# Diagonal sums of the sixth chunk on GpSimd, state scaling and the sums' copy on ScalarE, and a new order for the first chunks and weight loads

## The chip, the cores and the metric

The kernel runs on one core of one Trainium2 chip. The metric is the device time of one execution in microseconds (us). The kernel before was timed three times: 413.6, 413.74 and 414.51 us, median 413.74 us. The execution that was profiled took 413.68 us; from its first to its last instruction (the span, on which all times below are counted) are 412.0 us.

The engines are TensorE (PE: matmuls; PEld: its weight loads), VectorE (DVE), ScalarE (ACT), GpSimd (POOL) and SyncE (SP, which here only issues DMAs). Each works through its own instructions strictly in order.

## The reference

Two parts are chained. A linear attention with decay, per batch (4), head (8) and step (768), heads of width 48:

```
state = zeros(B, H, 48, 48)
for t in range(768):
    y[:, :, t] = r_t . (state + (u * k_t) outer v_t)
    state = w_t[:, None] * state + k_t outer v_t
```

Then, with x the 3072 rows of y with the heads side by side (384 wide), a gated layer: `h = max(x @ w1, x @ w2, x @ w3)` (768 wide), `out = h @ w_out`. Everything is float32; the weights w1, w2, w3 and w_out arrive as float64 bits.

## The kernel before, in words

The attention is cut into 24 chunks k of 128 steps (six per batch). A chunk has steps with one-letter names, and the number behind a letter is the chunk: `n` loads its r, k, w (tile `tin`, three buffers); `b`, `s`, `f` are VectorE's backward scan (L360), two tiny operations (L368, L369) and its forward scan (L374) of the decays; `r` scales r and k by them (L385, L386); `X` is the scores on TensorE (`gram`, L449); `T` transposes k (`tu`, L469, copied to `kn` by ScalarE, L471); `R` adds what comes from the state (L482); `U` makes the new state (L492, and L496, which adds the old one); `S` scales it by the decay `dec` into `sstar` (L507); `M` puts the scores under a mask into `a` (L458); `V` and `Z` multiply by v (L527); `E` copies the chunk's y into x (ScalarE, L545) and, after the third and fourth chunk, shifts 16-row pieces of x with six DMAs, three from SyncE's queue and three from ScalarE's (L554); `c` is a check of the decays on ScalarE (L391).

The diagonal term needs, per step and head, the sum over the width of u r k. For the first chunks (k < CS, here 6) step `d` multiplies r and k on VectorE (L399), `D` sums with small matmuls on TensorE (L411), and `e` copies the eight sums to `cs` (L419). For later chunks `d` is two multiplications on GpSimd of r, k and u loaded in another layout (`kr`, L402 and L403; u is `u_bc`), and `e` is a reduction on VectorE (L421). Either way GpSimd then spreads the sums over the diagonal of `a` (L427). Step `e` of chunk k also issues the load of v for chunk k+1 (and of `kr`, if it takes the GpSimd way) on SyncE's queue.

The layer works on halves of 512 rows (six in all). Every weight i of 24 takes a DMA (`w` or `load_w`, L287), one ScalarE operation (L303, it waits for the DMA) and two VectorE operations (L312, L314). For the first half plain float32 matmuls are used: the first two groups in two parts (L147 on 384 columns, L155 on the other 128), the rest whole (L167, six records a group). A group's sums lie in one of three `psm` buffers in turn (the sums of `D` and the warmers' matmuls use the same three), and are taken up one group later: the first by a copy on ScalarE (L130), the others by a maximum on VectorE (L133).

Order around the change: the string FRONT lists the first four chunks' steps one by one. `W4` is four warming matmuls on TensorE (L573) whose result nobody reads; `i` begins a weight (L303), `c` without a number begins and finishes one, `p` and `m` are a part or a group of matmuls of the layer, `w` loads a weight, `a` a unit of a later chunk. Each engine gets its part of this list in this order. SyncE's queue too: a DMA that must wait (for a buffer to come free, for x to be written, for an earlier DMA on one of the eight semaphores) holds up all behind it.

Of the kernel before, what the change touches and what calls it, by code (L numbers as in the profile page):

```python
# [34 lines left out]
ALU = mybir.AluOpType  # L35
AF = mybir.ActivationFunctionType
# [4 lines left out]
B, H, S, D = 4, 8, 768, 48  # L41
DM, FF = 384, 768
NP = 4
# [10 lines left out]
CPH = HT // C  # L54
# [12 lines left out]

FRONT = ("b0 s0 f0 d0 W2 D0 W3 r0 X0 T0 W3 c0 e0 b1 s1 d1 D1 U0 f1 W4 R0 e1 M0 V0 Z0 E0 S0 n3 r1 "  # L70
# [3 lines left out]
TURN = "b1 d1 w | f1 w | D1 r1 c1 | e1 M0 w | "  # L74
ORD = "w R0 V0 U0 X1 Z0 E0 b2 d2 | f2 n3 w | D2 S0 r2 c2 | e2 M1 w | T1 w | |"


START = ("mcamcamcamcamcamcaamca"
         "mcmacamcacammacmcamacamcamcamcamcamcaafafafaxmafmmammaaf")
CS = 6  # L80
LINE = 128
PLAIN = 1
CHECK = 2
# [11 lines left out]
def kernel(ctx: ExitStack, tc, tin, nat, u_flat, u_pair, v_t, w_all, out, ytr):  # L95
    nc = tc.nc
# [99 lines left out]
    with ExitStack() as fast:  # L196
# [23 lines left out]
        def load_nat(k):  # L220
            b, c = divmod(k, NCH)
            if k in natt:
                return
            vt = v_p.tile([128, DM], F32, name="v")
            kr = None
            if k >= CS:
                kr = nat_p.tile([128, 2, DM], F32, name="kr")
                nc.sync.dma_start(out=kr[:, :, :], in_=nat[b, c, :, 1:3, :])
            nc.sync.dma_start(out=vt[:, :], in_=nat[b, c, :, 0, :])
            natt[k] = (vt, kr)  # L230
# [39 lines left out]
        sstar = [cst.tile([128, NP, 64], F32, name=f"sstar{i}") for i in range(2)]  # L270
        dec = [cst.tile([128, LINE], F32, name=f"dec{i}")[:, 0:NP] for i in range(2)]
# [83 lines left out]
        prep = {k: {} for k in range(NK)}  # L355
# [37 lines left out]
        def prep_diag1(k):  # L393
            if k < CS:
                t = tbuf[k % NB]
                prep[k]["kr"] = n = nat_p.tile([128, 2, DM], F32, name="kr")[:, :, :].rearrange("p a b -> p (a b)")[:, 0:NP * C]
                n, r, q = (z.rearrange("p (a b) -> p a b", a=NP) for z in (n, t[:, WC:WC + NP * C], t[:, WC + NP * C:TC_]))
                for j in range(2):
                    nc.vector.tensor_tensor(out=pairs(n, j), in0=placed(r, j), in1=pairs(q, j), op=ALU.mult)  # L399
                return  # L400
            n = natt[k][1]
            nc.gpsimd.tensor_tensor(out=n[:, 0, :], in0=n[:, 0, :], in1=n[:, 1, :], op=ALU.mult)  # L402
            nc.gpsimd.tensor_tensor(out=n[:, 0, :], in0=n[:, 0, :], in1=u_bc[:, :], op=ALU.mult)  # L403

        def prep_diag_sum(k):
            if k < CS:
                n, t = prep[k]["kr"], tbuf[k % NB]
                prep[k]["ps"] = ps = ps_m.tile([128, HT], F32, name="psm")
                for pr in range(NP):
                    for lo in (0, HC):  # L410
                        nc.tensor.matmul(ps[lo:lo + HC, pr:2 * NP:NP], lhsT=n[0:112, pr * C + lo:pr * C + lo + HC],  # L411
                                         rhs=t[0:112, TC_ + 2 * pr:TC_ + 2 * pr + 2], start=(pr == 0), stop=True,
                                         skip_group_check=True)

        def prep_diag2(k):
            ahead("D", k)
            cs = small.tile([128, LINE], F32, name="cs")[:, 0:H]
            if k < CS:
                nc.vector.tensor_copy(out=cs[:, :], in_=prep[k]["ps"][:, 0:H])  # L419
            else:  # L420
                nc.vector.tensor_reduce(out=cs[:, :].rearrange("p (a b) -> p b a", a=2),  # L421
                                        in_=natt[k][1][:, 0, :].rearrange("p (b a d) -> p b a d", a=2, d=D),
                                        axis=AX.X, op=ALU.add)
            a = a_p.tile([128, 4, 3, HC], F32, name="a")
            for lo in (0, HC):
                rows = slice(lo, lo + HC)
                nc.gpsimd.affine_select(out=a[rows, :, 0:2, :], pattern=[[0, 4], [0, 2], [1, HC]],  # L427
                                        in_=cs[rows, :].rearrange("p (a b) -> p a b", b=2).unsqueeze(3).broadcast_to([HC, 4, 2, HC]),
                                        compare_op=ALU.is_equal, fill=0.0, base=0, channel_multiplier=-1)
            prep[k]["a"] = a  # L430
            if k + 1 < NK:
                load_nat(k + 1)
# [28 lines left out]
        def goes_on(k):  # L461
            return k % NCH < NCH - 1
# [36 lines left out]
        def state(k):  # L499

            if goes_on(k):
                new = prep[k]["pu"][0:112, 0:NP * D].rearrange("p (a b) -> p a b", a=NP)
                if k % NCH > 0 and k >= CPH:
                    cur = scur[0:112, :].rearrange("p (a b) -> p a b", a=NP)
                    nc.vector.tensor_tensor(out=cur, in0=new, in1=sstar[k % 2][0:112, :, 0:D], op=ALU.add)
                    new = cur
                nc.vector.tensor_tensor(out=sstar[(k + 1) % 2][0:112, :, 0:D], in0=new,  # L507
                                        in1=dec[(k + 1) % 2][0:112, :].unsqueeze(2).broadcast_to([112, NP, D]), op=ALU.mult)

        def after(later, sooner):  # L510

# [27 lines left out]
        def result(k):  # L539
# [11 lines left out]
            for lo in (0, 64) if cols else ():  # L551
                for j in range(KT):
                    eng = nc.scalar if lo and half < PLAIN else nc.sync
                    eng.dma_start(out=x[lo + 48:lo + 64, j, cols], in_=x[lo + 16 * j:lo + 16 * j + 16, KT, cols])  # L554

        steps = dict(X=scores, M=take, T=transposes, R=from_state, U=to_state, S=state, V=values, Z=values2, E=result, n=load,
                     b=prep_scan_b, s=prep_start, f=prep_scan_f, r=prep_rk, c=prep_check, d=prep_diag1,
                     D=prep_diag_sum, e=prep_diag2)
        ready = {("n", k) for k in range(3)}

        def ahead(step, k):

            if k < NK and (step, k) not in ready:
                ready.add((step, k))
                steps[step](k)
# [107 lines left out]
        def take_x(early=False):  # L673
            h = len(xs)
            there = ("E", CPH * (h + 1) - 2) in ready if early else units >= min(UPH * (h + 1) + XD, UPC * NK)
            if h < NH and there and groups >= GPH * h - 2 * CPH:
                xs[h] = x_parts(h)
# [39 lines left out]
        simple = dict(p=part, a=unit, c=weights, i=begin, w=load_w, m=group, f=fix, x=lambda: take_x(True))  # L717
        for step in FRONT.split():
            if step in simple:
# [14 lines left out]
    with tc.If(verdict[0] != 0, label="general"), ExitStack() as slow:  # L734
        pool = lambda name, bufs, **kw: slow.enter_context(tc.tile_pool(name=name, bufs=bufs, **kw))
        c1 = pool("c1", 1)
# [7 lines left out]
        with tc.For_i(0, B) as b:  # L744
            for pr in range(NP):
# [8 lines left out]
                for hh in range(2):  # L754
                    rows = slice(64 * hh, 64 * hh + 48)
                    for t, o in ((wt, pr * WS + 1), (rt, WC + pr * C), (kt, WC + NP * C + pr * C)):
                        for c in range(NCH):
                            for lo in (0, HC):
                                at = o + (HC - lo if t is kt and pr % 2 == 0 else lo)
                                nc.sync.dma_start(out=t[rows, c * C + lo:c * C + lo + HC],  # L760
                                                  in_=tin[ds(b, 1), c, rows, at:at + HC].rearrange("a p n -> (a p) n"))
                    nc.sync.dma_start(out=uc[rows, :], in_=u_pair[pr, hh])
                nc.vector.tensor_scalar(out=uk[0:112, :], in0=kt[0:112, :], scalar1=uc[0:112, :], scalar2=None, op0=ALU.mult)
                for j in range(KT):
                    with tc.For_i(0, 16) as i:
# [5 lines left out]
                        for hh in range(2):  # L771
                            nc.sync.dma_start(
                                out=vb[64 * hh:64 * hh + 48, :],
                                in_=v_t[ds(b, 1), 2 * pr + hh, ds(i + 16 * j, 1), :].rearrange("a e t -> (a e) t").broadcast_to([48, S]))
# [22 lines left out]
        for i in range(NW if w_all.dtype != F32 else 0):  # L797
# [5 lines left out]
            low, scale = raw[:, 0:2 * PC:2], sc[:, :].bitcast(F32)  # L803
# [16 lines left out]
        with tc.For_i(0, NH) as half:  # L820
            x = xs_p.tile([128, KT, HT], F32, name="x")
# [73 lines left out]
```

## Time and profile before

| what | value |
|---|---|
| median of three runs | 413.74 us |
| the profiled execution | 413.68 us |
| its span | 412.0 us |
| TensorE busy (matmuls) | 400.9 us, 97% |
| VectorE busy | 279.4 us, 68% |
| ScalarE busy | 151.3 us, 37% |
| GpSimd busy | 80.6 us, 20% |
| granted TensorE clock | 1.000 |

A line of the timeline gives the start in us, the duration, the engine, the line of the program, the operation, what it writes and reads, the shape, how many were merged, and in square brackets how long the engine sat idle before it and what ended that wait. "issue" is a wait that no semaphore in the profile explains. A line with SPq or ACTq is a DMA being issued. Matmuls overlap, so that busy time on TensorE includes time in the pipeline; merged lines of small matmuls end some 0.1 to 0.2 us after the next line starts.

### The profile page before, as it was taken

To read this page: it belongs to the slowest core of one execution; us is meant where nothing else is said; L and a number is where in the kernel's file an instruction comes from. 1 tells how busy PE (TensorE), PEld (TensorE's weight loads), DVE (VectorE), ACT (ScalarE), POOL (GpSimd) and SP (SyncE) were. 2 spreads that over 40 slices of the span, in tenths; PEclk is the share of its full clock that TensorE was granted. 3 is DMA by queue.
4 is the path that set the end of the run, shared out by engine and by line. 5 is a ranking of instruction groups with operands and counts; after the bars stand their busy time and mean duration, and the time that the engine had idled before them with its cause. 6 is when DMAs were issued, how large, how long until landed. Compare 5 with 4: busy or idle time off the path is not lost.

```text
span 412.0 us, 9165 instructions
## 1 busy us (share of the span) xinstructions
PE 400.9 (97%) x3729; PEld 315.6 (77%) x3729; DVE 279.4 (68%) x511; ACT 151.3 (37%) x318; POOL 80.6 (20%) x96
## 2 busy tenths in 40 slices
PE   6989999999999999999999999999999999999994
PEld 2656454556688889988889988889988888988894
DVE  6989999989869969848777658678666622233320
ACT  1344434233535532525433644433622321311211
POOL 2410032233222211213122212223123200000000
PEclk9999999999999999999999999999999999999999
DMA  8594994641550330595563686751550000300001
GB/s 210 157 324 143 335 312 140 208 139 40 152 176 23 105 111 17 139 286 163 176 184 113 158 267 212 228 154 43 180 168 2 0 2 2 97 1 0 2 15 66
DMA packets 24126, 54.09 MB, mean 131 GB/s; under 512 B 3312, under 2 KB 9776, under 8 KB 24080
## 3 DMA queue, kind: packets, MB, share of 16 engines
q1 hardware_dynamic: 20160, 43.43, 34.2%
q10 hardware_dynamic: 3920, 10.03, 8.1%
q8 instruction: 30, 0.49, 0.5%
q14 instruction: 16, 0.13, 0.1%
HBM read 47.55 MB, written 4.72 MB: 127 GB/s over the span
## 4 chain that ended last, share of the span: by engine, by line
PE 94%; DMA 1%; ACT 1%; issue 1%; SPq 1%; POOL 0%; POOLq 0%; ACTq 0%
PE psm L167 56%; PE psm L187 16%; PE gram L449 5%; PE y L527 5%; PE tu L492 3%; PE y L482 3%; PE psm L573 2%; PE tu L469 2%; DMA out_dram<-m 1%; PE psm L411 1%; PE psm L147 1%; SPq L554 1%; DMA x<-x 0%; PE psm L155 0%; PE tu L496 0%
## 5 line engine op out<-in xcount | busy, mean ns | idle before, releaser
L167 PE MATMUL psm<-x_hi,w 128*128 128x512 f32 x540 | 172.8, 394 | 0.2 <-ACT m L191 0.2
L167 PEld LDWEIGHTS psm<-x_hi,w 128*128 128x128 f32 x540 | 101.4, 188 | 22.0 <-ACT m L191 0.8
L167 PE MATMUL psm<-x_lo,w 128*128 128x512 f32 x270 | 105.3, 390 | 0.0
L133 DVE TENSOR_TENSOR m<-psm,m 128x512 f32<-128x512 f32 x60 | 41.1, 685 | 58.9 <-PE psm L167 44.5
L187 PE MATMUL psm<-w,h_hi 128*128 128x384 f32 x288 | 78.2, 364 | 0.0
L427 POOL TENSOR_SCALAR_AFFINE_SELECT a<-cs 64x512 f32<-64x512 f32 x48 | 37.1, 774 | 143.4 <-DVE cs L421 92.6
L167 PEld LDWEIGHTS psm<-x_lo,w 128*128 128x128 f32 x270 | 50.8, 188 | 9.8
L187 PEld LDWEIGHTS psm<-w,h_hi 128*128 128x128 f32 x288 | 51.8, 188 | 6.5 <-DVE w L314 0.4
L167 PE MATMUL psm<-x,w 128*128 128x512 f32 x96 | 42.6, 597 | 0.0
L545 ACT COPY x<-y 112x512 f32<-112x512 f32 x24 | 14.1, 586 | 75.2 <-PE y L527 74.7
L402 POOL TENSOR_TENSOR kr<-kr 128x384 f32<-128x384 f32 x18 | 21.1, 1172 | 99.8 <-PE y L527 88.5
L187 PE MATMUL psm<-w,h_lo 128*128 128x384 f32 x120 | 40.3, 336 | 0.0
L391 ACT ACTIVATE gf<-gf 112x1034 f32<-112x1034 f32 x24 | 25.7, 1070 | 35.6 <-DVE tin L386 35.2
L110 ACT CAST h_hi<-m 128x512 fp32r<-128x512 f32 x30 | 18.7, 622 | 53.7 <-DVE m L133 53.7
L374 DVE TENSOR_TENSOR_SCAN gf<-tin,d_fwd 112x517 f32<-112x517 f32 x24 | 36.1, 1502 | 0.7
L167 PEld LDWEIGHTS psm<-x,w 128*128 128x128 f32 x96 | 17.8, 190 | 20.4 <-issue 19.1
L360 DVE TENSOR_TENSOR_SCAN gf<-tin,d_bwd 112x517 f32<-112x517 f32 x24 | 29.9, 1246 | 4.8 <-DMA tin<-in_tin_dram 4.7
L111 DVE TENSOR_TENSOR h_lo<-m,h_hi 128x512 fp32r<-128x512 f32 x30 | 20.6, 688 | 16.7 <-ACT h_hi L110 16.7
L527 PE MATMUL y<-a,v 64*48 64x64 f32 (+3 forms) x768 | 25.7, 246 | 0.6 <-POOLq L534 0.2
L458 DVE COPY_PREDICATED a<-mask,gram 128x384 f32<-128x384 int32 x48 | 25.3, 581 | 0.5 <-PE gram L449 0.5
L527 PEld LDWEIGHTS y<-a,v 64*64 64x64 f32 (+1 forms) x768 | 21.6, 126 | 4.7 <-issue 3.1
L130 ACT COPY m<-psm 128x512 f32<-128x512 f32 x30 | 17.5, 582 | 16.4 <-PE psm L167 9.8
(72 smaller groups left out, 424.9 us busy)
## 6 DMA issues: line engine op xcount, KB each, us to landing
tin<-in_tin_dram SPq DMA_DIRECT2D x23, 448.0 KB, 5.1
w<-in_w_all_dram SPq DMA_DIRECT2D x24, 384.0 KB, 7.2
cv<-in_w_all_dram ACTq DMA_DIRECT2D x24, 384.0 KB, 3.6
kr<-in_nat_dram SPq DMA_DIRECT2D x18, 384.0 KB, 5.8
tin<-in_tin_dram SPq DMA_DIRECT2D x23, 231.0 KB, 3.5
v<-in_nat_dram SPq DMA_DIRECT2D x24, 192.0 KB, 5.5
out_dram<-m SPq DMA_DIRECT2D x24, 192.0 KB, 2.6
x<-x SPq DMA_DIRECT2D x30, 32.0 KB, 2.0
```

What stands on the lines that cost most here:

```text
L111: rest = lambda: nc.vector.tensor_tensor(out=lo, in0=src, in1=hi.bitcast(F32), op=ALU.subtract)
L133: nc.vector.tensor_tensor(out=m[:, :], in0=ps[:, :], in1=m[:, :], op=ALU.max)
L167: nc.tensor.matmul(ps[:, :], lhsT=wt[f * 3 + wi][:, ct * 128:(ct + 1) * 128], rhs=xt[:, ct, :], start=(n == 0), stop=(n == KT * len(terms) ...
L187: nc.tensor.matmul(pss[tt][:, 0:DM], lhsT=ht[f][:, tok], rhs=wt[FT * 3 + f][:, :], start=(f == 0 and i == 0), stop=(f == FT - 1 and i == l ...
L360: nc.vector.tensor_tensor_scan(out=gf[0:112, 0, ::-1], data0=t[0:112, 0:WC][:, ::-1], data1=d_bwd[0:112, ::-1], initial=0.0, op0=ALU.mult, ...
L374: nc.vector.tensor_tensor_scan(out=gf[0:112, 1, :], data0=tbuf[k % NB][0:112, 0:WC], data1=d_fwd[0:112, :], initial=0.0, op0=ALU.mult, op1 ...
L391: nc.scalar.activation(out=flat, in_=flat, func=AF.Square, accum_out=acc[0:112, k:k + 1])
L402: nc.gpsimd.tensor_tensor(out=n[:, 0, :], in0=n[:, 0, :], in1=n[:, 1, :], op=ALU.mult)
L427: nc.gpsimd.affine_select(out=a[rows, :, 0:2, :], pattern=[[0, 4], [0, 2], [1, HC]], in_=cs[rows, :].rearrange("p (a b) -> p a b", b=2).un ...
L449: nc.tensor.matmul(to, lhsT=p["kp"][q:q + 48, pr, lo:lo + HC], rhs=p["rp"][q:q + 48, pr, HC * late:C], start=(hh, lo) not in begun, stop=T ...
L458: nc.vector.copy_predicated(out=p["a"][:, 2 * hh:2 * hh + 2, :, :].rearrange("p a b c -> p a (b c)"), mask=mask_b(2), data=p["gs"][hh].rea ...
L527: mm = nc.tensor.matmul(p["y"][64 * half:64 * half + m, hh, j, HC * late:C], lhsT=natt[k][0][lo:lo + HC, h * D:h * D + m], rhs=a[:, j, :] ...
```

## The change

CS goes from 6 to 5, so that chunk 5 (the sixth) takes the GpSimd way. The copy of the sums (L419) goes from VectorE to ScalarE for the chunks that keep the TensorE way. The scaling of the state, one VectorE operation on 112x192, becomes four ScalarE operations on 112x48 for chunks 0 to 3 (k < CPH = 4). FRONT is written anew: `e` and `S` stand earlier, chunk 4's load `n4` stands behind the load of v4 and three weight loads instead of ahead of them, the third `i` stands behind `E2`, and the seven weight loads around the third and fourth chunk are spread differently (five stood ahead of `E2`, now four).

```diff
--- before.py
+++ after.py
@@ -67,17 +67,17 @@
 
 
 
-FRONT = ("b0 s0 f0 d0 W2 D0 W3 r0 X0 T0 W3 c0 e0 b1 s1 d1 D1 U0 f1 W4 R0 e1 M0 V0 Z0 E0 S0 n3 r1 "
-         "W2 X1 d2 D2 T1 c1 b2 s2 e2 R1 U1 M1 V1 Z1 E1 f2 S1 n4 w w w r2 "
-         "W4 X2 d3 D3 T2 c2 b3 s3 e3 w w R2 U2 n5 i i i M2 V2 Z2 E2 f3 S2 r3 "
-         "W3 X3 d4 T3 R3 M3 x V3 Z3 E3 w w U3 p p w w c n6 w m D4 b4 s4 c c3 S3 m w f4 c e4 m r4 c X4 T4 R4 c4 w w")
+FRONT = ("b0 s0 f0 d0 W2 D0 W3 r0 X0 e0 T0 W3 c0 b1 s1 d1 D1 U0 f1 W4 R0 e1 S0 M0 V0 Z0 E0 n3 r1 "
+         "W2 X1 d2 D2 e2 T1 c1 b2 s2 R1 U1 S1 M1 V1 Z1 E1 f2 r2 "
+         "W4 X2 d3 D3 e3 w w w n4 w T2 c2 b3 s3 R2 U2 S2 i i M2 V2 Z2 E2 i n5 f3 r3 "
+         "W3 X3 d4 T3 R3 M3 x V3 Z3 E3 w w w U3 p p w c n6 w m D4 b4 s4 c c3 S3 m w f4 c e4 m r4 c X4 T4 R4 c4 w w")
 TURN = "b1 d1 w | f1 w | D1 r1 c1 | e1 M0 w | "
 ORD = "w R0 V0 U0 X1 Z0 E0 b2 d2 | f2 n3 w | D2 S0 r2 c2 | e2 M1 w | T1 w | |"
 
 
 START = ("mcamcamcamcamcamcaamca"
          "mcmacamcacammacmcamacamcamcamcamcamcaafafafaxmafmmammaaf")
-CS = 6
+CS = 5
 LINE = 128
 PLAIN = 1
 CHECK = 2
@@ -416,7 +416,7 @@
             ahead("D", k)
             cs = small.tile([128, LINE], F32, name="cs")[:, 0:H]
             if k < CS:
-                nc.vector.tensor_copy(out=cs[:, :], in_=prep[k]["ps"][:, 0:H])
+                nc.scalar.copy(out=cs[:, :], in_=prep[k]["ps"][:, 0:H])
             else:
                 nc.vector.tensor_reduce(out=cs[:, :].rearrange("p (a b) -> p b a", a=2),
                                         in_=natt[k][1][:, 0, :].rearrange("p (b a d) -> p b a d", a=2, d=D),
@@ -504,8 +504,12 @@
                     cur = scur[0:112, :].rearrange("p (a b) -> p a b", a=NP)
                     nc.vector.tensor_tensor(out=cur, in0=new, in1=sstar[k % 2][0:112, :, 0:D], op=ALU.add)
                     new = cur
-                nc.vector.tensor_tensor(out=sstar[(k + 1) % 2][0:112, :, 0:D], in0=new,
-                                        in1=dec[(k + 1) % 2][0:112, :].unsqueeze(2).broadcast_to([112, NP, D]), op=ALU.mult)
+                for pr in range(NP) if k < CPH else ():
+                    nc.scalar.activation(out=sstar[(k + 1) % 2][0:112, pr, 0:D], in_=new[:, pr, :], func=AF.Identity,
+                                         scale=dec[(k + 1) % 2][0:112, pr:pr + 1])
+                if k >= CPH:
+                    nc.vector.tensor_tensor(out=sstar[(k + 1) % 2][0:112, :, 0:D], in0=new,
+                                            in1=dec[(k + 1) % 2][0:112, :].unsqueeze(2).broadcast_to([112, NP, D]), op=ALU.mult)
 
         def after(later, sooner):
```

On ScalarE, from the DMAs that shift x after the third chunk to the copy L130 that frees the first `psm` buffer of the layer (kn: the transposed k; dec: decay; cv: a weight on its way; gf: the decays). Before:

```order
L554 DMA x<-x 16x384 x3
L471 COPY kn<-tu 128x448
L545 COPY x<-y 112x4x128
L554 DMA x<-x 16x128 x3
L303 ACTIVATE cv<-w,minus_two 128x384
L362 COPY dec_137<-gf 112x4
L303 ACTIVATE cv<-w,minus_two 128x384
L391 ACTIVATE gf,acc<-gf 112x1034
L130 COPY h_hi<-psm 128x512
```

Now (lines are four higher from L512 on):

```order
L558 DMA x<-x 16x384 x3
L303 ACTIVATE cv<-w,minus_two 128x384
L471 COPY kn<-tu 128x448
L549 COPY x<-y 112x4x128
L558 DMA x<-x 16x128 x3
L303 ACTIVATE cv<-w,minus_two 128x384
L362 COPY dec_137<-gf 112x4
L303 ACTIVATE cv<-w,minus_two 128x384
L391 ACTIVATE gf,acc<-gf 112x1034
L508 ACTIVATE sstar_135<-tu,dec_137 112x48 x4
L130 COPY h_hi<-psm 128x512
```

One L303 (the third weight) now stands between the DMAs and kn, and the four scalings of chunk 3's state stand ahead of L130; the L303 just ahead of L391 is that of the fifth weight in both.

On SyncE's queue, from the load of v after the first chunk to the weights behind the shifts of x (tin: chunk inputs; w: weights; v: values; x<-x: the shifts of x). Before:

```order
L229 DMA v<-in_nat_dram 128x384
L241 DMA tin_115<-in_tin_dram 112x528
L241 DMA tin_115<-in_tin_dram 112x1024
L287 DMA w<-in_w_all_dram 128x384 x3
L229 DMA v<-in_nat_dram 128x384
L287 DMA w<-in_w_all_dram 128x384 x2
L241 DMA tin_116<-in_tin_dram 112x528
L241 DMA tin_116<-in_tin_dram 112x1024
L554 DMA x<-x 16x384 x3
L554 DMA x<-x 16x128 x3
L287 DMA w<-in_w_all_dram 128x384 x4
```

Now:

```order
L229 DMA v<-in_nat_dram 128x384 x2
L287 DMA w<-in_w_all_dram 128x384 x3
L241 DMA tin_115<-in_tin_dram 112x528
L241 DMA tin_115<-in_tin_dram 112x1024
L287 DMA w<-in_w_all_dram 128x384
L558 DMA x<-x 16x384 x3
L241 DMA tin_116<-in_tin_dram 112x528
L241 DMA tin_116<-in_tin_dram 112x1024
L558 DMA x<-x 16x128 x3
L287 DMA w<-in_w_all_dram 128x384 x4
```

The first three weights and chunk 4's tin have moved behind the load of v that waits for chunk 1's `Z`, the fifth weight has moved behind the shifts of x, and the first shifts have moved ahead of chunk 5's tin.

On VectorE, one turn (from chunk 2's decay operations to chunk 2's `r`; gram and a: scores; sstar: scaled state):

```order
@@ -28,8 +25,6 @@
 L368 TENSOR_SCALAR d_fwd<-gf 112x4
 L369 RECIPROCAL d_fwd<-d_fwd 112x4
-L419 COPY cs<-psm 128x8
 L458 COPY_PREDICATED a<-mask,gram 128x384 x2
 L374 SCALAR_TENSOR_TENSOR gf<-tin_116,d_fwd 112x517
-L507 TENSOR_TENSOR sstar_135<-tu,dec_137 112x4x48
 L385 TENSOR_TENSOR tin_116<-tin_116,gf 112x2x128 x2
 L386 TENSOR_TENSOR tin_116<-tin_116,gf 112x512
```

Each turn of the first chunks loses the small copy and the scaling; nothing else in it changes place.

## Rows read from the trace of the kernel before

**Rows 1.** The page's busy times of each engine, share of the span, instructions.

```profile
PE 400.9 (97%) x3729; PEld 315.6 (77%) x3729; DVE 279.4 (68%) x511; ACT 151.3 (37%) x318; POOL 80.6 (20%) x96
```

**Rows 2.** Timeline of TensorE: start, us, engine line op, count, [idle before].

```profile
19.07 0.67 PE L492 MATMUL tu<-v,kn 128*64 128x48 f32 x16
...
25.07 0.67 PE L492 MATMUL tu<-v,kn 128*64 128x48 f32 x14
27.09 0.29 PE L492 MATMUL tu<-v,kn 128*48 128x48 f32 x2 [1.35 <-issue]
...
33.16 0.86 PE L492 MATMUL tu<-v,kn 128*64 128x48 f32 x16
...
34.36 4.04 PE L147 MATMUL psm<-x,w 128*128 128x384 f32 x12
...
40.33 2.74 PE L167 MATMUL psm<-x,w 128*128 128x512 f32 x6
43.12 0.90 PE L449 MATMUL gram<-tin 48*64 48x128 f32 x32
...
52.99 0.63 PE L411 MATMUL psm<-tin,kr 112*64 112x2 f32 x16
53.55 5.42 PE L167 MATMUL psm<-x,w 128*128 128x512 f32 x12
58.90 0.50 PE L527 MATMUL y<-a,v 64*64 64x128 f32 x12
```

**Rows 3.** Timeline of VectorE, one turn and after the layer's first groups.

```profile
18.45 0.14 DVE L419 COPY cs<-psm 128x8 f32<-128x8 f32 x1
...
20.60 0.32 DVE L507 TENSOR_TENSOR sstar<-tu,dec 112x192 f32<-112x192 f32 x1
20.84 0.90 DVE L385 TENSOR_TENSOR tin<-tin,gf 112x256 f32<-112x256 f32 x2
...
40.60 0.69 DVE L133 TENSOR_TENSOR h_hi<-psm,h_hi 128x512 f32<-128x512 f32 x1 [0.25 <-PE psm L155]
...
42.38 0.68 DVE L386 TENSOR_TENSOR tin<-tin,gf 112x512 f32<-112x512 f32 x1
```

**Rows 4.** DMA view of 24.6 to 25.4 us: queue, packets, MB, share.

```profile
q8 instruction: 1, 0.02, 7.4%
```

**Rows 5.** Timeline of SyncE's queue: DMA issues.

```profile
18.80 0.79 SPq L241 DMA_DIRECT2D tin<-in_tin_dram  x2
19.64 1.37 SPq L287 DMA_DIRECT2D w<-in_w_all_dram  x3
21.47 0.33 SPq L229 DMA_DIRECT2D v<-in_nat_dram  x1
...
29.73 5.86 SPq L554 DMA_DIRECT2D x<-x  x6
35.63 2.00 SPq L287 DMA_DIRECT2D w<-in_w_all_dram  x4
```

**Rows 6.** Timeline of ScalarE from the third chunk's y to the first L130.

```profile
29.12 0.58 ACT L545 COPY x<-y 112x512 f32<-112x512 f32 x1 [1.13 <-PE y L527]
29.73 2.80 ACTq L554 DMA_DIRECT2D x<-x  x3
32.58 0.53 ACT L471 COPY kn<-tu 128x448 f32<-128x448 f32 x1 [2.87 <-PE y L482]
33.21 0.59 ACT L545 COPY x<-y 112x512 f32<-112x512 f32 x1
...
36.61 0.65 ACT L303 ACTIVATE cv<-w,minus_two 128x384 f32<-128x384 uint32 x1
37.16 1.05 ACT L391 ACTIVATE gf<-gf 112x1034 f32<-112x1034 f32 x1
...
39.10 0.58 ACT L130 COPY h_hi<-psm 128x512 f32<-128x512 f32 x1 [0.80 <-PE psm L155]
...
46.93 0.36 ACTq L577 DMA_DIRECT2D u_bc<-in_u_flat_dram  x1
```

**Rows 7.** DMA issues of 35.6 to 36.2 us: KB, us from issue to landing.

```profile
w<-in_w_all_dram SPq DMA_DIRECT2D x1, 384.0 KB, 3.4
```

**Rows 8.** DMA issues of 46.5 to 47.5 us, the same columns.

```profile
u_bc<-in_u_flat_dram ACTq DMA_DIRECT2D x1, 192.0 KB, 7.2
```

**Rows 9.** The page's costliest groups: count, busy us, mean ns, idle before.

```profile
L402 POOL TENSOR_TENSOR kr<-kr 128x384 f32<-128x384 f32 x18 | 21.1, 1172 | 99.8 <-PE y L527 88.5
```

## The prediction

> **What bounds the kernel now.** I read the page's busy times first: TensorE is busy 97% of the span, VectorE 68%, ScalarE 37%, GpSimd 20% [rows 1]. Then TensorE's timeline, to see where that 97% is real work at full rate. From 34.36 us on it is: the layer's matmuls follow each other without a wait worth naming [rows 2], so a microsecond that TensorE gains or loses up to about 43 us, where chunk 4's scores follow the layer's third group, comes out at the end whole, and so does TensorE work removed later. Before 34.36 us TensorE is filled with warming matmuls, and VectorE's chain of scans sets the pace together with it. One thing there is a plain hole: the matmuls of chunk 2's U start at 25.07, 14 of 16 records run, and the last two wait 1.35 us until 27.09, for nothing that a semaphore shows [rows 2]. The same step of chunk 1, at 19.07, has no such hole [rows 2]. So the question is: how much sooner do the first four chunks end, and does TensorE keep that.
>
> **The small copy and the scaling leave VectorE.** In a turn VectorE loses the copy of the sums (0.14 us at most) and the scaling, whose start at 20.60 is 0.24 us ahead of the next operation at 20.84 [rows 3]: about 0.3 us a turn, three turns before chunk 3. TensorE gets less of it, because its warmers fill each turn to within 0.1 us or so of VectorE's; from the turns' order I take 0.2 us in all up to chunk 2's U. Bounds: 0 (TensorE keeps its pace) and 0.9 (all of it).
>
> On ScalarE four operations on 112x48 from PSUM have no row. Nearest rows: 0.53 us for a 448-column copy from PSUM, 0.59 us for one of 512 [rows 6]. Four of those would be 2.1 to 2.4 us, the upper bound; the lower is 0 (hidden in a wait, which holds for chunks 0 to 2, where the state is wanted a whole turn later). The time that goes with the columns should shrink about ninefold, so I take 0.5 us for four. This is paid only for chunk 3, whose four stand ahead of L130.
>
> [...]
>
> **The hole at 25.5 us.** What fills it? In the DMA view one packet of the instruction queue q8, 0.02 MB, stands at 24.6 to 25.4 us [rows 4], just ahead of the wait. And chunk 3's U takes 0.86 us against 0.67 [rows 2], a smaller hole one turn later. I read both as TensorE waiting for its own next block of instructions, whose packet came late because from 18.80 us on chunk 4's tin and three weights lay in the DMA queues ahead of it [rows 5]. The order now is: v4 (issued at 21.47 [rows 5], when chunk 1's Z is through), then three weights, then chunk 4's tin. So from about 18 to 21 us the queues are empty, and a block asked for around 19 comes at once. I take the hole as gone: 1.35 us, and about 0.2 us of pipeline filled again, 1.55 in all. Bounds: 0 and 1.6. The next block is then fetched while the queues are full, as the one before 33.16 was; a wait of 0.2 to 1.2 us in chunk 3's U is likely again, but stands beside the wait that comes next.
>
> [...]
>
> **From chunk 2's y to the third group: a new wait.** Chunk 2's y copy E2 ended at 29.70 (29.12 + 0.58 [rows 6]). Now: 1.55 and 0.2 sooner, but 0.3 later because the scaling and two L303 stand ahead of it on ScalarE: about 28.25. Then three DMA issues, 2.80 us before [rows 6]; they ended as the queues ran empty, I take 2.3, so 30.55. Now comes the third L303, moved here: 0.55 (36.61 to 37.16 [rows 6]), then kn 0.53, and the y copy of chunk 3 ends near 32.05, against 33.80 before (33.21 + 0.59 [rows 6]). The layer's first matmul, 0.57 us behind that before, starts at about 32.7, 1.65 us sooner. TensorE would reach its third group 5.97 us later (34.36 to 40.33 [rows 2]), at 38.7.
>
> It cannot start there. The group's sums go to the `psm` buffer of the first group, which ScalarE frees by L130. Before, L130 ran at 39.10, as soon as TensorE was done, ScalarE having idled 0.80 us [rows 6]. Now the L303 of the fifth weight stands ahead of it, and that weight's load has moved behind the shifts of x on SyncE's queue. Before, what stood behind the shifts (the sixth weight) was issued at 35.63, 1.83 us after that y copy [rows 5, 6], and landed 3.4 us later [rows 7]. So the fifth now lands at 32.05 + 1.83 + 3.4 = 37.3. Behind it on ScalarE: L303 0.55, the check L391 with its accumulator read 1.1, four scalings 0.5, L130 0.58: 40.05, plus a semaphore, 40.1. Before, the third group started at 40.33 [rows 2]. Of 1.65 us that the front wins, 0.2 are left; the rest is a wait of TensorE of 1.4 us on ScalarE. VectorE's next maximum (L133) also waits for L130, and chunk 4's r behind it, 2.46 us from 40.60 to 43.06 [rows 3]; so the scores at 43.12 [rows 2] come at 42.6 to 42.9. I keep 0.25 us won. Bounds: lost 0.5 (weight lands 0.7 later, or the scalings take 1.2), won 1.8 (nothing waits).
>
> **Chunk 5 leaves TensorE.** Its 16 matmul records go from 52.99 to 53.55 [rows 2]: 0.56 us, in a stretch where TensorE has no gaps, so all of it counts. In their place GpSimd multiplies twice, 1.17 us each [rows 9], and VectorE reduces. The second multiply needs u_bc, issued at 46.93 [rows 6] and landed 7.2 us later [rows 8], at 54.1; with 1.17 for it and an estimated 0.6 for the reduction the sums are there at about 55.9, the masked scores some 1.1 us later, 57, and TensorE wants them at 58.90 - 0.8 = 58.1 [rows 2]. That is 1 us of cover; without it each microsecond of delay would cost one. [...] I take 0, bounds 0 and 0.6 lost.
>
> **Sum**, against the profiled execution's own 413.68 us: -0.25 - 0.56 = -0.81, which gives 412.87. The median of the runs is 0.06 above the profiled one: 412.9.
>
> **Rivals.**
> 1. *Everything won is kept.* If the fifth weight lands two microseconds sooner than I think or TensorE does not meet the full buffer, the third group starts 1.5 to 1.7 us sooner: 413.74 - 1.6 - 0.56 = 411.6. For: ScalarE had 0.80 us to spare ahead of L130 [rows 6]. Against: the order of both queues is fixed, and the load cannot be issued before the shifts. 0.18.
> 2. *The wait eats a little more.* Fifth weight 0.4 to 0.7 us later, or the scalings at 0.25 us each: third group 0.3 to 0.6 later than before, 413.74 + 0.45 - 0.56 = 413.6, no change. For: the load of u_bc, with others in the queue, took 7.2 us [rows 8]. Against: before, the load in the same place took 3.4 [rows 7]. 0.17.
> 3. *Slower: the hole stays.* If the 1.35 us are not a late block, or the block is still late at this place, E2 ends at 29.70 - 0.2 + 0.3 = 29.8, and everything behind it, up to L130, carries the moved L303 (0.55), the wait for the fifth weight and the scalings as worked out above: the third group starts at 28.25 to 29.8 = 1.55 later than in the forecast, 41.65, which is 1.3 us later than before. With 0.3 us of the bounds on load and scalings used, 1.6: 413.74 + 1.6 - 0.56 = 414.8. It decides from the point where the whole hole stays and 0.1 us of those bounds comes on top. [...] Against: the packet just ahead, and a second, smaller hole at the same step. 0.15.
>
> **How the numbers follow.** My forecast has 0.50, the rivals 0.18, 0.17 and 0.15. About 0.2% (0.83 us) is what a measurement of this kernel can tell from no change; the forecast at -0.8 lies on that edge, so its own range, 412.3 to 413.4, is split in halves: 0.25 faster, 0.25 same. Faster: 0.25 + 0.18 = 0.43. Same: 0.25 + 0.17 = 0.42. Slower: 0.15. The range must reach to rival 1 and to the near side of rival 3: 411.4 to 414.3.
>
> **What would show it.** In the new timeline: no idle time in chunk 2's L492 near 25 us; the layer's first L147 at 32 to 33 us instead of 34.36; then a wait of TensorE of 1 to 2 us ahead of the first L167, released by ScalarE's L130, which itself follows an L303 that waited for a weight's DMA until about 37.3; the next scores at 42.6 to 42.9; no L411 between the groups near 53 us; no new TensorE wait near 58. I am wrong if the hole is still there, if L167 starts at once behind L155, or if a wait opens at chunk 4's V.

## The result and the profile after

The changed kernel takes 417.98 us (median of 5 runs, 416.3 to 419.73) against 413.74 (5 runs, 412.65 to 414.51): the ratio is 1.0104, 95% interval 1.0067 to 1.0142. It is 1% slower; the forecast was 412.9 with a range up to 414.3. (All ratios here leave disturbed runs out, so they can differ a little from the quotient of two medians.) The profiled execution took 418.78 us, 5.1 more than that of before; its span is 417.1, the mean granted clock 0.988 against 1.0.

TensorE's timeline after (start, us, engine line op, count, [idle before <- what ended it]), to be laid beside [rows 2]:

```profile
24.34 0.67 PE L492 MATMUL tu<-v,kn 128*64 128x48 f32 x16
...
27.36 0.90 PE L449 MATMUL gram<-tin 48*64 48x128 f32 x32
...
32.69 2.43 PE L531 MATMUL y<-a,v 64*64 64x128 f32 x32 [3.31 <-DVE a L458]
35.05 1.09 PE L492 MATMUL tu<-v,kn 128*64 128x48 f32 x16
...
36.84 4.96 PE L147 MATMUL psm<-x,w 128*128 128x384 f32 x12
...
45.12 4.54 PE L167 MATMUL psm<-x,w 128*128 128x512 f32 x6 [1.22 <-ACT h_hi L130]
49.59 0.90 PE L449 MATMUL gram<-tin 48*64 48x128 f32 x32
...
64.61 0.56 PE L531 MATMUL y<-a,v 64*64 64x128 f32 x16
```

Two more rows of the timeline before, chunk 3's scores and its V:

```profile
29.73 0.90 PE L449 MATMUL gram<-tin 48*64 48x128 f32 x32
...
31.59 1.55 PE L527 MATMUL y<-a,v 64*48 64x128 f32 x32
```

Chunk 2's U runs through without its hole. Chunk 3's scores start at 27.36 and not, as before, at 29.73: the front is 2.37 us ahead. Then chunk 3's V waits 3.31 us for VectorE, a wait that stood nowhere in the forecast. The layer's first group starts at 36.84, not 34.36; the third group waits for L130, as forecast, but at 45 us instead of 40; chunk 4's scores come 6.47 us later (49.59 against 43.12). From there to the end the changed kernel is 1.4 us shorter.

Why VectorE was late, in its timeline after:

```profile
26.54 0.68 DVE L386 TENSOR_TENSOR tin<-tin,gf 112x512 f32<-112x512 f32 x1
31.38 0.76 DVE L399 TENSOR_TENSOR kr<-tin 112x256 f32<-112x256 f32 x2 [4.16 <-DMA x<-x]
32.06 1.04 DVE L458 COPY_PREDICATED a<-mask,gram 128x384 f32<-128x384 int32 x2
```

L399 is chunk 4's products for its diagonal sums (step d4). It needs chunk 4's tin, and it stands ahead of L458, chunk 3's masking (M3), for which TensorE's V waits. The row names x<-x, the last DMA event before; what L399 waits for is the tin, as its landing shows. Before, the same L399 ran 1.8 us sooner and did not wait:

```profile
29.54 0.75 DVE L399 TENSOR_TENSOR kr<-tin 112x256 f32<-112x256 f32 x2
```

SyncE's queue after, and the issues of 22.6 to 23.6 us in the DMA view (KB, us from issue to landing):

```profile
15.47 5.76 SPq L229 DMA_DIRECT2D v<-in_nat_dram  x2
21.28 1.38 SPq L287 DMA_DIRECT2D w<-in_w_all_dram  x3
22.76 0.84 SPq L241 DMA_DIRECT2D tin<-in_tin_dram  x2
```

```profile
tin<-in_tin_dram SPq DMA_DIRECT2D x1, 448.0 KB, 8.1
```

Before, the tin was issued at 18.80 [rows 5] and its larger half landed 3.9 us after its issue, at 23.1. Now that half, the second of the two DMAs that start at 22.76, is issued at about 23.2, behind v4 and three weights, and takes 8.1 us: it lands at 31.3, just where L399 starts.

The windows of after (us, busy us of each engine with its operations, granted clock, DMA share, GB/s) show a second price:

```profile
32.00:38.00 6.00, 5.22 (x52) 4.10 (x53) 5.65 (x12) 0.59 (x1) 0.00 (x0) 0.50 0.46 124
...
45.00:49.00 4.00, 3.88 (x5) 1.64 (x6) 3.87 (x6) 1.30 (x4) 1.65 (x2) 0.57 1.06 257
```

After TensorE's idle time at 29.4 the granted clock is 0.50 from 32 to 38 us, and 0.57 from 45 to 49, behind the wait for L130. L147's twelve matmuls take 4.96 us instead of 4.04, the third group 4.54 instead of 2.74.

ScalarE's timeline after, to [rows 6]:

```profile
42.14 0.64 ACT L303 ACTIVATE cv<-w,minus_two 128x384 f32<-128x384 uint32 x1 [2.34 <-DMA w<-in_w_all_dram]
42.69 1.05 ACT L391 ACTIVATE gf<-gf 112x1034 f32<-112x1034 f32 x1
...
43.74 0.85 ACT L508 ACTIVATE sstar<-tu,dec 112x48 f32<-112x48 f32 x4
44.47 0.60 ACT L130 COPY h_hi<-psm 128x512 f32<-128x512 f32 x1
```

This is the chain of the forecast, link by link: the fifth weight's L303 waits for its load, then L391, four scalings in 0.85 us (0.5 had been taken), then L130, and TensorE behind it.

So at chunk 4's scores: 2.37 won in the front; 3.47 lost by V3's start relative to chunk 3's scores (5.33 us behind them, 1.86 before); 1.38 for V3, U3 and the adding of the old state (L496) at a clock of 0.50; 0.93 in L147; 1.38 ahead of the third group; 1.68 in it at the lower clock (0.57): -2.37 + 8.84 = 6.47.

### The profile page after: what moved, and what is told of

Same layout as the page of the kernel before. It is cut to its first block, busy times and chain, and to the rows that moved or that the text cites. A ratio compares the mean times of both kernels' runs of the same rounds, so it can differ in the third digit from the quotient of the medians.

```text
span 417.1 us, 9154 instructions
## 1 busy us (share of the span) xinstructions
PE 403.7 (97%) x3713; PEld 317.2 (76%) x3713; DVE 279.1 (67%) x500; ACT 155.0 (37%) x339; POOL 81.7 (20%) x98
## 4 chain that ended last, share of the span: by engine, by line
PE 90%; DMA 4%; ACT 2%; SPq 2%; issue 1%; POOL 0%; DVE 0%; POOLq 0%; ACTq 0%
PE psm L167 55%; PE psm L187 16%; PE y L531 5%; PE gram L449 4%; PE tu L492 3%; PE y L482 3%; DMA w<-in_w_all_dram 2%; PE psm L577 2%; PE tu L469 2%; SPq L558 1%; DMA x<-x 1%; DMA out_dram<-m 1%; PE psm L411 0%; ACT x L549 0%; ACT x_hi L110 0%
## 5 line engine op out<-in xcount | busy, mean ns | idle before, releaser
L167 PE MATMUL psm<-x,w 128*128 128x512 f32 x96 | 44.1, 617 | 1.2 <-ACT h_hi L130 1.2
L391 ACT ACTIVATE gf<-gf 112x1034 f32<-112x1034 f32 x24 | 25.7, 1069 | 36.1 <-DVE tin L386 35.7
L374 DVE TENSOR_TENSOR_SCAN gf<-tin,d_fwd 112x517 f32<-112x517 f32 x24 | 36.2, 1506 | 0.7
L167 PEld LDWEIGHTS psm<-x,w 128*128 128x128 f32 x96 | 18.4, 196 | 23.2 <-issue 20.9
L458 DVE COPY_PREDICATED a<-mask,gram 128x384 f32<-128x384 int32 x48 | 25.3, 581 | 0.0
L130 ACT COPY m<-psm 128x512 f32<-128x512 f32 x30 | 17.5, 582 | 14.6 <-PE psm L167 11.0
```

The costliest lines, as they stand in the source:

```text
L167: nc.tensor.matmul(ps[:, :], lhsT=wt[f * 3 + wi][:, ct * 128:(ct + 1) * 128], rhs=xt[:, ct, :], start=(n == 0), stop=(n == KT * len(terms) ...
L374: nc.vector.tensor_tensor_scan(out=gf[0:112, 1, :], data0=tbuf[k % NB][0:112, 0:WC], data1=d_fwd[0:112, :], initial=0.0, op0=ALU.mult, op1 ...
L391: nc.scalar.activation(out=flat, in_=flat, func=AF.Square, accum_out=acc[0:112, k:k + 1])
L458: nc.vector.copy_predicated(out=p["a"][:, 2 * hh:2 * hh + 2, :, :].rearrange("p a b c -> p a (b c)"), mask=mask_b(2), data=p["gs"][hh].rea ...
```

## The experiments

Each ratio is to runs of the kernel before on the same chip in the same batch: 413.59 us (21 runs) for the first four, 413.80 (17) for the next four, 414.39 (25) for the last. Theory: the tin behind v4 and the weights makes d4, and with it M3 and V3, late; the fifth weight makes the second wait; the low clock behind both idle times (0.50 and 0.57 in the changed kernel) comes from them. Rival: the move of work to ScalarE is itself the loss. The groups were run on different chips, so a difference of medians across groups is rough.

**1. d4 behind the layer's first two parts.**

```diff
-W3 X3 d4 T3 R3 M3 x V3 Z3 E3 w w w U3 p p w c
+W3 X3 T3 R3 M3 x V3 Z3 E3 w w w U3 p p d4 w c
```

> The changed kernel with one move on VectorE: d4 (chunk 4's first multiplication of r and k, which waits for chunk 4's tin) stands behind the layer's first two parts instead of ahead of chunk 3's M; the DMA order stays. Theory A (late tin: VectorE stands 4.16 us in d4, M3 and so TensorE's V3 wait behind it, and the halved clock follows from TensorE's idle time): V3's 3.31 us wait is gone, clock 1.00 throughout, the layer's first L147 at 32 to 33 us, then a wait for L130 of about 1 us ahead of the third group as forecast at first; 412.3 to 413.8 us. Theory B (ScalarE has too much to do; the scalings, copies and moved L303 hold up TensorE): V3 or U3 still waits, 416 us or more.

Measured: 416.43 us, ratio 1.0073 [1.0040, 1.0106]: not the 412.3 to 413.8 that was expected. V3 starts at 29.21 without a wait, so d4 was what held it. But another hole opens one step later, and the clock falls behind it (0.50 from 34 to 36 us):

```profile
33.70 0.99 PE L492 MATMUL tu<-v,kn 128*64 128x48 f32 x16 [2.95 <-issue]
...
42.24 2.84 PE L167 MATMUL psm<-x,w 128*128 128x512 f32 x6
```

It names no semaphore, like the hole of before in chunk 2's U. An instruction packet (queue q8 of the DMA view) comes at 31.0 us here; more on that under 12. The wait at the third group is gone, as the front is late again: L130 ends at 42.19, just ahead of it.

**2. The tin ahead of v4.**

```diff
-W4 X2 d3 D3 e3 w w w n4 w T2
+W4 X2 d3 D3 n4 e3 w w w w T2
```

> The changed kernel with one move on SyncE's queue: chunk 4's tin is loaded ahead of v4 and the first weights again (as soon as chunk 1's buffer is free, near 18.5 us); VectorE's order stays. Theory A (late tin): d4 does not wait, V3's wait is gone, clock 1.00, 412 to 414 us; whether the 1.35 us hole of the kernel before comes back tells if one tin of 0.7 MB in the queues is enough to delay TensorE's block of instructions (then 413.5 to 414.5) or the three weights were needed (412 to 413). Theory B (ScalarE's burden): 416 us or more.

Measured: 415.17 us, ratio 1.0022 [0.9984, 1.0059]; profiled 413.26. TensorE:

```profile
29.09 1.54 PE L531 MATMUL y<-a,v 64*48 64x128 f32 x32
31.50 0.67 PE L492 MATMUL tu<-v,kn 128*64 128x48 f32 x16 [0.88 <-ACT kn L471]
...
32.52 4.04 PE L147 MATMUL psm<-x,w 128*128 128x384 f32 x12
...
40.86 2.84 PE L167 MATMUL psm<-x,w 128*128 128x512 f32 x6 [2.21 <-ACT h_hi L130]
```

V3's wait is gone and so is the low clock behind it (1.0 from 32 to 38 us). What remains is the mechanism of the forecast: first L147 at 32.52 (forecast 32 to 33), then a wait for L130 that eats the gain, and more than the gain: the third group starts 0.53 us later than before. By the medians this order of issues on one queue is 2.8 us of the 4.2. Its runs spread from 412.49 to 417.92 us, with clocks of 1.0 down to 0.988; whether the wait for L130 costs clock in some executions is not shown, as only one of them, at 1.0, was profiled.

**3 and 4. Code and order crossed.** The third kernel is the changed one with FRONT of before; the fourth is the kernel before with the new FRONT and nothing else.

> The changed kernel with the order string FRONT of the kernel before: only chunk 5's way, the copy of the sums and the scaling of the state are changed. Theory A (late tin): no wait in d4, the 1.35 us hole in chunk 2's U is back, clock 1.00, 412.8 to 413.6 us (0.56 us of chunk 5's sums gone). Theory B (ScalarE's burden): 415 us or more, with TensorE waiting for ScalarE in the first four chunks. Theory C (chunk 5 on GpSimd is late, u_bc lands too late): a wait of TensorE at chunk 4's V near 58 us, 414 us or more.

> The kernel before with only the new FRONT: VectorE still copies the sums and scales the state, chunk 5's sums stay on TensorE. Theory A (late tin): the wait of some 4 us in d4 is there with all that follows, no hole in chunk 2's U, 417 to 419.5 us. Theory B (ScalarE's burden): no large wait, 413 to 414 us.

Measured: 417.78 us, 1.0078 [1.0041, 1.0115], and 421.18 us (four runs, 416.22 to 423.29; the first was profiled), 1.0199 [1.0151, 1.0248]. Neither half alone is any good. In the fourth, chunk 1 loses a microsecond at V, as chunk 2 does at 28.78:

```profile
21.09 1.73 PE L527 MATMUL y<-a,v 64*64 64x128 f32 x32 [1.01 <-DVE a L458]
```

The scaling, now written ahead of M, keeps VectorE from M while it waits for the state; d4's wait for the tin is down to 1.07 us, as the front comes later. The third kernel's one profile is of its longest run (419.65). In it the rival holds: the scaling of chunk 2's state, now on ScalarE, stands in the old order behind E2's three shifts of x, and TensorE's next step (T3) waits for it.

```profile
32.55 0.88 ACT L508 ACTIVATE sstar<-tu,dec 112x48 f32<-112x48 f32 x4 [3.21 <-issue]
```

```profile
33.48 1.01 PE L469 MATMUL tu<-ident,tin 112*128 112x112 f32 x4 [2.67 <-ACT sstar L508]
```

How long that wait is in the other runs is not shown. So order and ScalarE's new work belong together.

**5. Eleven warming matmuls in V3's wait.**

```diff
-W3 X3 d4 T3 R3 M3 x V3
+W3 X3 d4 T3 R3 W11 M3 x V3
```

> The changed kernel with eleven more warming matmuls (22 TensorE instructions) between chunk 3's R and V, where TensorE waited 3.31 us for VectorE. Nothing that V3 waits for is touched, so V3 should still start at 32.5 to 32.9 us. Theory (the late tin costs twice: the wait itself and the halved clock that follows an idle TensorE): the granted clock of 32 to 38 us, 0.50 before, should be 1.0; V3/Z3, U3 and the layer's first group then run at full rate, the first L147 starts near 35.8 instead of 36.84 and L167 near 43.2 to 43.9, 1.2 to 1.9 us sooner; the end 1.5 to 3 us sooner, 415 to 416.5. Rival (the half clock has another cause, such as the load of the layer's own start): the clock falls at the same place all the same, and the time stays at 417.5 to 418.5.

Measured: 419.19 us, 1.0131 [1.0090, 1.0172]. Inconclusive, since the wait itself grew: V3 at 33.40, with 1.67 us still idle, and the clock fell behind it (0.70 and 0.50 from 34 to 38 us).

**6. Tin and fifth weight early.**

```diff
-W4 X2 d3 D3 e3 w w w n4 w T2 ... E3 w w w U3
+W4 X2 d3 D3 n4 e3 w w w w w T2 ... E3 w w U3
```

> The changed kernel with chunk 4's tin ahead of v4 (as in the second experiment) and the fifth weight's load also ahead of chunk 2's E, so that ScalarE's fifth L303 no longer waits for it. Theory (the two moved loads are the whole of the loss): neither V3 nor the third group waits; L303 at about 35.1, L130 when TensorE is done with the buffer at about 38.4, L167 at 38.5 to 39.2 (40.86 with the tin alone), X4 at 41.4 to 42.2 against 43.12 in the kernel before; the profiled time 411 to 412, the median 411.5 to 413.5. Rival (the third group is held by ScalarE's work ahead of L130, not by the weight): L167 still near 40.5 and the time as with the tin alone, about 413.3 profiled, 415 median.

Measured: 412.04 us, 0.9957 [0.9934, 0.9981]: faster than before. On ScalarE L130 now waits for TensorE and no longer for a weight; on TensorE one wait is left, and a low clock behind it (0.72 from 32 to 38 us), which is why chunk 4's scores come at 43.00 and not at the expected 41.4 to 42.2:

```profile
39.10 0.59 ACT L130 COPY h_hi<-psm 128x512 f32<-128x512 f32 x1 [1.65 <-PE psm L155]
```

```profile
31.75 0.79 PE L492 MATMUL tu<-v,kn 128*64 128x48 f32 x16 [1.02 <-ACT kn L471]
...
33.24 5.15 PE L147 MATMUL psm<-x,w 128*128 128x384 f32 x12
...
43.00 0.90 PE L449 MATMUL gram<-tin 48*64 48x128 f32 x32
```

**7. The fifth weight early, the tin left late** (`e3 w w w n4 w w T2`, and one w fewer ahead of U3).

> The changed kernel with the fifth weight's load put behind chunk 4's tin, ahead of chunk 2's E, and the tin left where the change has it. Theory: V3 still waits about 3.3 us for VectorE (d4 for the tin), the clock is still halved behind it, but L167 follows L155 at once; L167 1.2 to 2.5 us sooner than in the changed kernel's 45.12, the time 415.5 to 417. Rival (the wait at the third group is only there because the clock is low or the front is late): no gain, 417.5 to 418.5.

Measured: 416.48 us, 1.0070 [1.0047, 1.0093]. V3 still waits, the third group does not:

```profile
33.46 2.43 PE L531 MATMUL y<-a,v 64*64 64x128 f32 x32 [4.33 <-DVE a L458]
...
44.24 2.74 PE L167 MATMUL psm<-x,w 128*128 128x512 f32 x6
46.92 0.90 PE L449 MATMUL gram<-tin 48*64 48x128 f32 x32
```

By the medians against 417.98, the weight alone is worth 1.5 us, the tin alone 2.8, both 5.9 (417.98 - 412.04). That is 1.6 more than the sum, for which the traces show one reason, that with the tin early TensorE meets the weight's wait earlier and longer (2.21 us against 1.22); but the interval of 2 alone is some 1.5 us to either side, so the difference is not clear of noise.

**8. As 6, and kn ahead of the third L303.**

```diff
-M2 V2 Z2 E2 i n5 f3 r3 W3 X3 d4 T3 R3 M3
+M2 V2 Z2 E2 n5 f3 r3 W3 X3 d4 T3 R3 i M3
```

> As the run before last (tin and fifth weight early), and the third L303 moved on ScalarE from ahead of the copy kn of chunk 3 to behind it. Chunk 3's U waited 0.88 us for kn with the tin early; kn comes 0.55 us sooner, so U3 about 0.5 us sooner, at 31.0, and the rest with it: 0.3 to 0.5 us below the kernel with tin and weight early. Rival: the third weight's low part comes 0.5 us later at VectorE, and VectorE's r4 and the layer's third matmul take it back: no difference.

Measured: 410.47 us, 0.9919 [0.9888, 0.9949], the best of all and faster than both kernels. Half a microsecond less of waiting brings three times as much or more:

```profile
29.18 1.54 PE L531 MATMUL y<-a,v 64*48 64x128 f32 x32
31.27 0.67 PE L492 MATMUL tu<-v,kn 128*64 128x48 f32 x16 [0.55 <-ACT kn L471]
...
32.28 4.04 PE L147 MATMUL psm<-x,w 128*128 128x384 f32 x12
...
41.36 0.90 PE L449 MATMUL gram<-tin 48*64 48x128 f32 x32
...
56.38 0.56 PE L531 MATMUL y<-a,v 64*64 64x128 f32 x16
```

V3 stands at the same place as in 6 (29.19); chunk 4's scores come 1.64 us sooner, of which 0.47 is the wait and 1.2 the clock, which stays at 1.0 here.

**9. Eighteen warming matmuls** (W18 where 5 had W11).

> As the kernel with eleven warming matmuls in the wait ahead of V3, now with eighteen (the eleven had ended 1.67 us before V3 and the clock still fell at 34.6 us). V3 is still released by VectorE's M3 at 32.7 to 33.5 us. Theory (an idle TensorE halves the clock, and that is a cost beside the wait): the granted clock stays 1.0 from 30 to 40 us, V3/Z3 take 1.55 instead of 2.43, L147 starts 2.6 to 3.0 us behind V3 instead of 4.15; the third group is then held by L130 at about 43.2 to 44.2, 1 to 2 us sooner than in the changed kernel; the time 415.5 to 417.2. Rival (only the waits count): the third group starts near 45 all the same, the time is 417.5 or more.

Measured: 419.25 us, 1.0113 [1.0088, 1.0137]. A miss: V3 came at 34.78, 2.1 us later than in the changed kernel. The tin's larger half took 10.1 us here, against 8.1. Nor did the clock stay at 1.0 up to 40 us, as expected: it is 1.0 up to 36 us, then 0.78 and 0.50 up to 40, and L147 takes 5.40 us. Even so, chunk 4's scores come 14.4 us after V3 (49.17) against 16.9 in the changed kernel. Of these 2.5 us, 1.2 lie between V3 and L147, and 1.6 in the third group, which runs at a clock of 1.0 here (44 to 50 us). That the time is no shorter is then the later tin; whether the added matmuls delay it, or the load only varies, is open.

**10. As 8, chunk 5's sums back on TensorE** (CS = 6).

> The best kernel so far (tin and fifth weight early, kn first: 410.5 us) with chunk 5's diagonal sums back on TensorE. Theory (the 0.56 us of 16 matmuls in a stretch without gaps come back whole): 0.4 to 0.7 us slower, 410.9 to 411.2. Rival (chunk 5's sums on GpSimd and VectorE cost as much through the load of kr and the late u_bc): no difference or faster, 410.0 to 410.5.

Measured: 412.21 us, 0.9958 [0.9932, 0.9983]; 0.39% more than 8, some 1.6 us. In the trace:

```profile
41.62 0.90 PE L449 MATMUL gram<-tin 48*64 48x128 f32 x32 [0.15 <-DVE tin L386]
...
51.49 0.63 PE L411 MATMUL psm<-tin,kr 112*64 112x2 f32 x16
...
57.40 0.56 PE L531 MATMUL y<-a,v 64*64 64x128 f32 x16
```

From chunk 4's scores to its V it is 15.78 us, in 8 it is 15.02: 0.76 for matmuls whose row had shown 0.56 [rows 2]. In 8 no wait opens at that V, so nothing of it is lost through GpSimd. The rest of the difference lies ahead (0.26 at chunk 4's scores) and in the spread of the runs.

**11. As 8, but the copy of the sums and the scaling on VectorE, as before the change.**

> The same best kernel with the copy of the sums and the scaling of the state back on VectorE, as before the change; order, loads and chunk 5 as in the best one. Theory from the run of the new order alone (there the scaling on VectorE, now ahead of M, made TensorE's V wait about 1 us in two chunks): 1 to 3.5 us slower, 411.5 to 414, with waits of TensorE's V for VectorE's L458 in chunks 1 and 2. Rival (the prediction's price of edit a, 0.2 us): 410.5 to 410.9.

Measured: 416.64 us, 1.0064 [1.0030, 1.0098]: by the ratios 1.5%, some 6 us, more than 8, well over the 3.5 that the theory had allowed. TensorE's V waits 1.01 us for L458 in chunks 1 and 2, as expected. The clock falls as well (0.61 from 22 to 24 us, 0.50 from 34 to 38), in a profile that is longer than the median (419.25), so the 6 us are not waits alone. VectorE's timeline says where the waits come from:

```profile
27.11 0.17 DVE L419 COPY cs<-psm 128x8 f32<-128x8 f32 x1 [2.13 <-PE psm L411]
27.20 1.23 DVE L360 TENSOR_TENSOR_SCAN gf<-tin,d_bwd 112x517 f32<-112x517 f32 x1
...
29.56 0.36 DVE L507 TENSOR_TENSOR sstar<-tu,dec 112x192 f32<-112x192 f32 x1 [0.43 <-PE tu L496]
```

The copy takes 0.17 us and waits 2.13 for TensorE's sums, with the scan of the next chunk queued behind it; the scaling waits again. On ScalarE the copy waits as well (1.81 us in 6), and it holds up nobody: there TensorE is 0.91 to 1.00 busy in each microsecond from 22 to 30. (That is the price in this order; in that of before, the copy came later and did not wait [rows 3].)

**12. The kernel before, with three weights issued behind v4, and e3 earlier.**

```diff
-f2 S1 n4 w w w r2 W4 X2 d3 D3 T2 c2 b3 s3 e3 w w R2
+f2 S1 r2 W4 X2 d3 D3 n4 e3 w w w T2 c2 b3 s3 w w R2
```

> The kernel before, with only chunk 4's tin and three weights issued later on SyncE: behind D3 and around v4, at about 21.5 to 24 us, not at 18.8 to 21. Theory (the hole of 1.35 us in chunk 2's U is a late instruction block behind these loads): no idle in chunk 2's U, the first L147 at 32.8 to 33.3 instead of 34.36, the third group at 38.9 to 39.6 instead of 40.33, the profiled time 412.2 to 412.8, the median some 1 us below that of the kernel before. Rival (the hole is not due to these loads, or only moves to the next block): a hole of 1 us or more in chunk 2's or 3's U, and no gain.

Measured: 414.21 us, 1.0015 [0.9981, 1.0048]: no gain. The edit did not do what had been meant. The tin is issued at 18.36, no later than before; only the three weights went behind v4. And e3, which issues v4's load, was moved ahead of b3 with it, so that its copy of the sums on VectorE waits for TensorE, with the scan behind it:

```profile
23.48 0.17 DVE L419 COPY cs<-psm 128x8 f32<-128x8 f32 x1 [0.90 <-PE psm L411]
```

The hole is gone, and at the third group 0.1 us is left of it.

```profile
24.64 0.67 PE L492 MATMUL tu<-v,kn 128*64 128x48 f32 x16
...
29.12 0.90 PE L449 MATMUL gram<-tin 48*64 48x128 f32 x32 [0.62 <-DVE tin L386]
...
34.20 4.11 PE L147 MATMUL psm<-x,w 128*128 128x384 f32 x12 [0.58 <-DMA x<-x]
...
40.24 2.74 PE L167 MATMUL psm<-x,w 128*128 128x512 f32 x6
```

VectorE's r is late for chunk 3's scores by 0.62 us, less than the 0.90 that e3 costs, and ScalarE's L303, ahead of the copy that feeds the shifts of x, waits for the weights that are now late. So this run does not tell what the hole alone is worth.

What the hole is, the DMA view tells better. In the kernel before an instruction packet comes at 24.6 us [rows 4], and TensorE goes on at 27.09, some 2.4 us later; in 1 it comes at 31.0, and TensorE goes on at 33.70, some 2.6 later. In the other twelve profiles, and for this U in 1 too, the packet ahead of chunk 2's U came 2.5 us or more before that U started, and there is no hole. So a late block of instructions fits every profile. That the loads in the queue make it late is not shown: in 3 they are issued as in the kernel before (the tin at 19.59), and the packet comes at 21.6, in time.

```profile
27.26 0.65 ACT L303 ACTIVATE cv<-w,minus_two 128x384 f32<-128x384 uint32 x1 [0.98 <-DMA w<-in_w_all_dram]
```

## Why the prediction was wrong

**The step that failed** is the one on the hole: "The order now is: v4 ..., then three weights, then chunk 4's tin. So from about 18 to 21 us the queues are empty". The move was priced only by what it frees. The other side, who waits for the moved load, was not asked for the tin, though it was asked for the fifth weight. The rows were there: the tin issued at 18.80, v4 at 21.47 [rows 5], three loads of 384 KB in between. d4 stood ahead of M3 on VectorE before the change too, but it ran at 29.54, when its tin had been there for 6 us. Experiments 1, 2 and 6 show it: taking d4 away or bringing the tin forward removes V3's wait, and with the tin, the fifth weight and kn all early (8) the same operations are faster than the kernel before.

**A cost that had no term** is the clock. Each idle spell of TensorE in the forecast was priced at its own length. In the changed kernel's trace V3's wait goes with a clock of 0.50 from 32 to 38 us, and 7 against 8 gives the price: from V3 to chunk 4's scores 13.46 us with the clock at 0.51 from 32 to 38 us, 12.18 with it at 1.0, and the latter holds a wait of 0.55 which 7 has not: 1.8 us. In the kernel before, too, the time goes with the clock from run to run: in the last batch its five runs at clocks of 0.988 to 0.990 took 415.29 to 416.84 us, the ten at 0.999 to 1.0 412.13 to 413.76.

**Right, by the trace:** the hole in chunk 2's U goes away, and its packet comes at 19.8 us, as forecast; from that U to chunk 3's scores it is 3.02 us instead of 4.66, 1.64 less where 1.55 had been taken. TensorE waits for L130 behind the fifth weight (2.21 us in experiment 2 where 1.4 had been worked out, 1.22 in the changed kernel). No wait opens at chunk 4's V.

**Near by luck.** The profile of experiment 2 (413.26) lies close to the forecast of 412.9, but not by its sum: the third group starts 0.53 us later than before, which is the second rival's picture, and chunk 4's scores 0.65 later, where 0.25 sooner had been forecast; the stretch from there to the end is 1.15 us shorter, where 0.56 had been taken. The end of chunk 2's y copy (28.20, forecast 28.25) is two misses that cancel: V2 starts 2.38 us sooner (25.44 against 27.82), where 1.75 had been taken, and the copy starts 2.19 us behind it instead of 1.30, where 0.3 more had been taken for the scaling and two L303.

**Wrong in size:**
- Copy and scaling off VectorE: 0.2 us had been taken up to chunk 2's U, from busy time; that U starts 0.73 us sooner (24.34 against 25.07 [rows 2]). How much of this is the moved work and how much the new order was not separated. What this work costs on VectorE in the new order, 4 and 11 show: waits for TensorE.
- The fifth weight: its load had been put 1.83 us behind chunk 3's y copy; in experiment 2 it is issued at 34.56, 2.62 us behind it, and its L303 starts 3.3 us later, as forecast (3.4).
- The four scalings: 0.85 us, between the bounds of 0 and 2.4.
- Chunk 5 off TensorE: 0.56 had been taken, 0.76 is there between chunk 4's scores and its V.

The first rival, that everything won is kept, has come true in experiment 8 (third group at 38.62, 1.71 us sooner than before), but only with the tin, a weight's load and one L303 put elsewhere.

## What to carry to other kernels

When an order changes, list for every moved load both who follows it in the queue and which instruction first reads what it brings, and what stands behind that instruction on its engine; a load that was early by 6 us has no row that says so. What a small operation costs can be its wait rather than its busy time: in 11 a copy of 0.17 us held VectorE's queue for 2.13. A wait of TensorE can cost more than its length: from 6 to 8 it went from 1.02 to 0.55 us, and chunk 4's scores came 1.64 us sooner, so halves of a microsecond ahead of a dense stretch can be worth moving. And an edit that moves one step in such a list moves all that the step does, as e3 in 12: look in the new trace whether what was meant to move did.

## What the runs showed of the hardware

The granted clock fell to 0.50 behind waits of TensorE of 4.33, 3.31, 2.95, 1.67, 1.24 and 1.02 us (7, the changed kernel, 1, 5, 9 and 6) and stayed at 1.0 behind 0.88 and 0.55 (2 and 8); from 6 to 8, 0.47 us of waiting made a difference of 1.64. But it also stayed up behind the 1.35 us hole in the profile of the kernel before and behind 2.21 us in that of 2, and behind waits of 1.01 us it stayed up in 4 (mean 0.999) and fell in 11 (0.61 from 22 to 24 us): length alone does not decide, and no run here shows what does.

The same load of 448 KB took 3.7 to 5.2 us from issue to landing where it was issued ahead of v4 and the weights (before, 2, 3, 6, 8, 10, 11, 12), and 7.1 to 10.1 behind v4 and three weights (the changed kernel, 1, 4, 5, 7, 9).

TensorE stopped without a named semaphore for 1.35 us (before) and 2.95 us (1), and went on some 2.4 and 2.6 us after an instruction packet had come.
